# A fused complex-decay attention and feed-forward kernel: unit 0's attention reordered, stacking issued by two queues, one scale step moved

## The chip, the cores and the metric

The kernel runs on one core of one Trainium2 chip. The metric is device time of one execution in microseconds. A profiled execution adds a span, from its first to its last recorded instruction, and a trace of every engine: PE (matrix products), DVE and ACT (element-wise work), POOL, and SP, whose queue here only issues DMAs. ACT has a DMA queue of its own too.

## What is computed

```python
def _attn_ref(q, k, v, a_re, a_im):                  # [4, 8, 768, 48] each
    mag = np.sqrt(a_re * a_re + a_im * a_im)
    scale = np.minimum(mag, 0.999) / (mag + 1e-06)
    a_re_n, a_im_n = (a_re * scale, a_im * scale)
    for t in range(S):
        ar, ai = (a_re_n[:, :, t, :, None], a_im_n[:, :, t, :, None])
        new_re = ar * S_re - ai * S_im
        new_im = ar * S_im + ai * S_re
        kv = np.einsum('bhd,bhe->bhde', k[:, :, t], v[:, :, t])
        S_re, S_im = (new_re + kv, new_im)
        y[:, :, t] = np.einsum('bhd,bhde->bhe', q[:, :, t], S_re)

def _moe_ref(x, w_a, w_b, w_out):                    # x: the attention's output, 3072 x 384
    return ((x @ w_a) * (x @ w_b) @ w_out)           # 384 -> 1536 -> 384
```

## The kernel before

The recurrence is computed in chunks of 128 tokens. A **unit** is one chunk of two batches (256 tokens, eight heads of 48): 12 units, six chunks for each of two pairs of batches. For every unit `u` the program does this:

- `load_a(u)` brings the decays (`a_t`, one of two buffers), `load_qk(u)` the queries and keys, `load_v(u)` the values; all on SP's queue.
- `scale(u, a_t, tmp)` computes the factor by which the decays are scaled. It is a chain between ACT and DVE: squares (L178), a sum (DVE, L179), four transcendental passes and a square (ACT, L180 to L184), then DVE's L186, ACT's L187, and DVE's L189, L191 and L193. `tmp` is a tile whose contents are no longer needed. Five DVE passes in all.
- `prep(u)` multiplies the decays by that factor (L211), forms cumulative products of them (L227 to L302), and turns queries and keys into decayed ones: L318 to L324 for the keys, and twice L309, which ends it. It is a generator: the main loop draws pieces of it between products.
- `stack(u)` copies the result from `qk` into `stk`, one DMA per head (two heads straddle a 128-partition border and take two), ten in all. Heads 0 to 7 are issued in order.
- `attn(u)` works from `stk`, for each batch `i` of the two and each half `hg` of the heads: `scores` (L379, four products into a `pm` bank, then DVE's mask into a tile `am`, L382), `transposes` of the keys (L390, copied to `kt` by ACT, L394), `outputs` (L422, values times masked scores plus the carried state, into `xp`; ACT casts it to `xh`, L424), `residual` (what the cast lost, to `xl`: for units 0 and 1 by a product L432 and ACT's L435, later by DVE's L430), and `state` (L445 and L452 to L456, the carried state `us`).
- The feed-forward of unit `w` runs over 12 blocks `f` of the hidden width: `gemm1` is 18 products (L489) into a bank `ab`; ACT and DVE turn that into `hh` and `hl` (L497 to L500); `gemm2`, two blocks later, is six products (L507).

Before the loop, unit 0 is prepared alone, and the weights are converted to a pair of tiles each (`split_weights`: DVE's L134 to L138, ACT's L142 and L149, PE's L147 and L148), 36 pieces; what is left of them is spread over w=0. In iteration `w` of the main loop the products of unit `w`, attention of unit `w+1` and `prep` of later units are written interleaved; a scheduler that knows priorities (`tc.high_priority`) then fixes one order for each engine, and each engine and each DMA queue works through its own in order, waiting where an operand isn't there.

In `prep`, the scale of the next unit is drawn along with the rounds of the cumulative product: `prep(1)` runs scale(1) ahead of itself and scale(2) within its last rounds, `prep(2)` runs scale(3), and so on. The attention of unit 0 has an order of its own, written at the end of `attn`. The pools give `am` two buffers, `xh` and `xl` two, `pm` two banks, `ab` three.

Of the kernel before, what the change touches and what calls it, by code (L numbers as in the profile page):

```python
# [8 lines left out]
F32 = mybir.dt.float32  # L9
# [13 lines left out]
NU = NBP * NCH  # L23
# [17 lines left out]
RUN = 2 * TOK + 2  # L41
NF = DF // 128
KS = 2 * D
LAG = 2
HB = 3
OWN_FROM = 2
# [21 lines left out]
def tile_kernel(ctx: ExitStack, tc: tile.TileContext, a_d, qk_d, v_d, w_d, qn_d, kn_d, vn_d, an_d, out_d):  # L68
    nc = tc.nc
    vec, act, pe, sync = nc.vector, nc.scalar, nc.tensor, nc.sync  # L70
# [8 lines left out]
    kvp = fast.enter_context(tc.tile_pool(name="kvp", bufs=2))  # L79
# [26 lines left out]
    stk = const.tile([128, H, RUN], F32, name="stk")  # L106
    nc.gpsimd.memset(stk[KS:128], 0.0)
    qk = const.tile([128, NJ, 2, RUN], F32, name="qk")
# [46 lines left out]
    def load_a(u):  # L155
        t = apool.tile([128, 2, W], F32, name="a_t")
        for hs in halves if u == 0 else (slice(0, W),):
            sync.dma_start(out=t[:, :, hs], in_=a_d[u, :, :, hs])
        return t

    a_tiles = {}

    sc_tiles = {}
    halves = (slice(0, W // 2), slice(W // 2, W))
# [2 lines left out]
    def scale(u, a_t, tmp):  # L167

        sc = zpool.tile([128, W], F32, name="sc")
        for n, hs in enumerate(halves if u == 0 else (slice(0, W),)):
            n = n and NU
            t = tmp[:, 0:2, hs]
            m, x, s0 = t[:, 0], t[:, 1], sc[:, hs]
            act.activation(out=t, in_=a_t[:, :, hs], func=AF.Square, accum_out=sums[:, u + n:u + n + 1])  # L178
            vec.scalar_tensor_tensor(out=m, in0=m, scalar=-EPS * EPS, in1=x, op0=ALU.add, op1=ALU.add)  # L179
            act.activation(out=s0, in_=m, func=AF.Ln, bias=b_sq)  # L180
            act.activation(out=s0, in_=s0, func=AF.Exp, scale=0.5)
            act.activation(out=s0, in_=s0, func=AF.Ln, bias=b_eps)
            act.activation(out=s0, in_=s0, func=AF.Exp, scale=-1.0)
            act.activation(out=x, in_=s0, func=AF.Square)  # L184
            yield 900
            vec.tensor_tensor(out=m, in0=m, in1=x, op=ALU.mult)  # L186
            act.activation(out=x, in_=s0, func=AF.Identity, scale=-EPS, bias=b_one)  # L187
            yield 900
            vec.scalar_tensor_tensor(out=m, in0=m, scalar=-0.5, in1=x, op0=ALU.mult, op1=ALU.add)  # L189
            yield 900  # L190
            vec.scalar_tensor_tensor(out=s0, in0=m, scalar=0.5, in1=s0, op0=ALU.add, op1=ALU.mult)  # L191
            yield 900
            vec.scalar_tensor_tensor(out=s0, in0=s0, scalar=0.999, in1=x, op0=ALU.mult, op1=ALU.min)  # L193
            yield 900
        sc_tiles[u] = sc
# [4 lines left out]
    def prep(u):  # L200
        c = u % NCH
        a_t = a_tiles.pop(u)
        if u == 1:
            yield from scale(u, a_t, a_first)
            a_tiles[u + 1] = load_a(u + 1)
        sc = sc_tiles.pop(u)
        z = zpool.tile([128, 3, W], F32, name="z") if u else z_first
# [4 lines left out]
                              in1=sc.rearrange("p (b i e) -> p b i e", e=2, i=SUB // 2), op=ALU.mult)  # L212
        act.activation(out=z[:, 0], in_=z[:, 2], func=AF.Copy, scale=-1.0)
        yield 1700
        sg = scale(u + 1, a_tiles[u + 1], a_t) if 0 < u < NU - 1 else iter(())


        zb = z.rearrange("p s (j b e) -> p s j b e", j=SUB // 2, e=2)
# [5 lines left out]
        for i in range(1, SUB):  # L224
            pr = small.tile([128, 2, 2, NB], F32, name="pr", bufs=1)
            for o, n in parts:
                vec.tensor_tensor(  # L227
                    out=pr[:, :, :, o:o + n],
# [7 lines left out]
        for _ in sg:  # L236
# [9 lines left out]
            out=pt, in0=last2[1],  # L246
# [13 lines left out]
        for sb in range(0, NSB, 2):  # L260
            pb = small.tile([128, 2, 2, G], F32, name="pb")
            vec.tensor_tensor(  # L262
                out=pb,
# [9 lines left out]
            out=pt, in0=last2[0], in1=bv[:, 1:3, 0:NB:2].unsqueeze(1).broadcast_to([128, 2, 2, NB // 2]), op=ALU.mult)  # L273
# [12 lines left out]
        for k in range(2):  # L286
            pz = a_t
            for s in range(2):
                vec.tensor_tensor(  # L289
                    out=pz[:, s].rearrange("p (j b e) -> p j b e", j=SUB // 2, e=2), in0=zb[:, 1 + s],  # L290
# [38 lines left out]
        for k in range(2):  # L329
            times_p(k, 0 if u else 1, 2)  # L330
            yield 1670
        if 0 < u < NU - 2:
            a_tiles[u + 2] = load_a(u + 2)

    def load_qk(u):
        sync.dma_start(out=qk[:, :, 1, 0:2 * TOK], in_=qk_d[u])

    def stack(u):
        n = RUN if rescaled(u % NCH) else 2 * TOK
        for h in range(H):  # L340
            r0 = h * D
            while r0 < (h + 1) * D:
                j, p = divmod(r0, 128)
                m = min((h + 1) * D - r0, 128 - p)
                d0 = 2 * (r0 - h * D)
                sync.dma_start(out=stk[d0:d0 + 2 * m, h, 0:n], in_=qk[p:p + m, j, :, 0:n])
                r0 += m


# [12 lines left out]
                          (3 * g + 2, [(2 * g, 32), (2 * g + 1, 64)])):  # L362
            quads[q % 4].append((q // 4, [(h, g * 128 + off) for h, off in pieces]))

    def attn(u, xh, xl):

        c = u % NCH
        last = c + 1 == NCH
# [5 lines left out]
        def scores(i, hg):  # L374
            qs, ks = cols(i)
            sp = ps_m.tile([128, 4, 128], F32, name="pm")
            for h4 in range(4):
                h = hg * 4 + h4
                pe.matmul(out=sp[:, h4], lhsT=stk[:, h, ks], rhs=stk[:, h, qs], start=True, stop=True)  # L379
            am = kvp.tile([128, 512], F32, name="am", bufs=2).rearrange("p (h t) -> p h t", h=4)  # L380
            with tc.high_priority(offset=ATTN_FIRST):
                vec.tensor_tensor(out=am, in0=sp, in1=mask[:].unsqueeze(1).broadcast_to([128, 4, 128]),  # L382
                                  op=ALU.mult)
            ams[i, hg] = am

        def transposes(i, hg):
            qs, ks = cols(i)
            tp = ps_m.tile([128, 512], F32, name="pm")
            for h4 in range(4):
                pe.transpose(out=tp[:, h4 * KS:(h4 + 1) * KS], in_=stk[0:KS, hg * 4 + h4, ks],  # L390
                             identity=ident[0:KS, 0:KS])
            kt = kvp.tile([128, 4, KS], F32, name="kt", bufs=2)
            with tc.high_priority(offset=ATTN_FIRST):
                act.copy(out=kt.rearrange("p h k -> p (h k)"), in_=tp[:, 0:4 * KS])  # L394
            kts[i, hg] = kt
# [41 lines left out]
        def state(i, hg):  # L437
# [4 lines left out]
            for h4 in range(4):  # L442
                h = hg * 4 + h4
                o = (h // 2) * 128 + (h % 2) * (80 if own else 32)
                pe.matmul(out=kp[0:KS, h4 * n:(h4 + 1) * n], lhsT=kts[i, hg][:, h4, :],  # L445
                          rhs=v_t[:, o:o + n], start=True, stop=True)
# [3 lines left out]
            with tc.high_priority(offset=ATTN_FIRST):  # L450
# [4 lines left out]
                if rescaled(c):  # L455
                    vec.tensor_tensor(out=uv, in0=uv, in1=sv, op=ALU.mult)  # L456

        order = [(scores, 0, 0), (scores, 0, 1), (transposes, 0, 0), (transposes, 0, 1),
                 (outputs, 0, 0), (scores, 1, 0), (residual, 0, 0), (state, 0, 0), (scores, 1, 1),
                 (state, 0, 1), (transposes, 1, 0), (transposes, 1, 1), (outputs, 1, 0),  # L460
                 (state, 1, 0), (residual, 1, 0), (state, 1, 1)]
        if u == 0:
            order = [(scores, 0, 0), (scores, 0, 1), (outputs, 0, 0), (scores, 1, 0), (scores, 1, 1),
                     (residual, 0, 0), (outputs, 1, 0), (transposes, 0, 0), (transposes, 0, 1),
                     (residual, 1, 0), (state, 0, 0), (state, 0, 1), (transposes, 1, 0), (transposes, 1, 1),
                     (state, 1, 0), (state, 1, 1)]
        for fn, i, g in order:
            if not (last and fn in (transposes, state)):
                fn(i, g)
# [5 lines left out]
    def new_x():  # L475
        return (moe.tile([128, NJ, TOK], F32, name="xh"), moe.tile([128, NJ, TOK], F32, name="xl"))
# [126 lines left out]
                    sync.dma_start(out=out_v[bass.ds(c, 1), bp, tt].rearrange("o p m -> p (o m)"), in_=o_sb)  # L603


    a_first = a_tiles[0] = load_a(0)
    load_weights(0)
    load_qk(0)
    load_weights(1)
# [21 lines left out]
    p1 = prep(1)  # L631
    for _ in range(CONV_FIRST):
        next(ws)
    x_cur = new_x()
    for _ in attn(0, *x_cur):
        drain(p1, P1_A)
    pend = []

# [11 lines left out]
    for w in range(NU):  # L650
# [18 lines left out]
        for f in range(NF):  # L669
# [9 lines left out]
            slot()  # L679
            if len(pend) > LAG:  # L680
                second()
# [11 lines left out]
        x_cur = x_nxt  # L693
# [74 lines left out]
```

## Time and profile before

| | |
|---|---|
| median of 3 runs | 691.08 us (691.05 to 691.49) |
| the profiled execution | 690.18 us |
| its span | 688.5 us |
| PE busy | 644.5 us, 94% of the span |
| DVE busy | 550.1 us, 80% |
| ACT busy | 310.1 us, 45% |
| stack(0), stack(1), stack(2) start | 57.63, 121.20, 167.64 us |

Busy shares are averages over the span. Rows of the timeline give start, duration, engine, line, operation, output and inputs, and in brackets the idle time of the engine ahead of it with what ended it. An engine's next instruction can start a little before the one ahead of it ends. A product of 32-bit operands outside the feed-forward shows as two records.

### The profile page before, as it was taken

To read this page: it belongs to the slowest core of one execution; us is meant where nothing else is said; L and a number is where in the kernel's file an instruction comes from. 1 tells how busy PE (TensorE), PEld (TensorE's weight loads), DVE (VectorE), ACT (ScalarE), POOL (GpSimd) and SP (SyncE) were. 2 spreads that over 40 slices of the span, in tenths; PEclk is the share of its full clock that TensorE was granted. 3 is DMA by queue.
4 is the path that set the end of the run, shared out by engine and by line. 5 is a ranking of instruction groups with operands and counts; after the bars stand their busy time and mean duration, and the time that the engine had idled before them with its cause. 6 is when DMAs were issued, how large, how long until landed. Compare 5 with 4: busy or idle time off the path is not lost.

```text
span 688.5 us, 14290 instructions
## 1 busy us (share of the span) xinstructions
PE 644.5 (94%) x5842; PEld 608.3 (88%) x5842; DVE 550.1 (80%) x1259; ACT 310.1 (45%) x622; POOL 5.6 (1%) x11
## 2 busy tenths in 40 slices
PE   3547999999999999999999999999999999999996
PEld 1214889899999999999999999999999999999996
DVE  6999899998989989999898898999989963233221
ACT  7357664735445346354363553635542332221221
POOL 3000000000000000000000000000000000000000
PEclk9676999999999999999999999999999999999999
DMA  8963301513314225043160440611500500400000
GB/s 321 402 268 95 121 1 44 143 54 87 115 39 139 63 78 145 16 136 104 29 194 2 122 117 3 178 60 62 155 24 18 153 24 18 108 24 2 24 1 28
DMA packets 30232, 63.94 MB, mean 93 GB/s; under 512 B 3664, under 2 KB 7248, under 8 KB 30160
## 3 DMA queue, kind: packets, MB, share of 16 engines
q1 hardware_dynamic: 26704, 58.23, 27.3%
q10 hardware_dynamic: 3456, 4.72, 1.9%
q8 instruction: 48, 0.79, 0.5%
q14 instruction: 24, 0.20, 0.1%
HBM read 39.32 MB, written 4.72 MB: 64 GB/s over the span
## 4 chain that ended last, share of the span: by engine, by line
PE 66%; DVE 25%; ACT 4%; DMA 2%; issue 2%; SPq 0%; DVEq 0%; ACTq 0%
PE ab L489 33%; PE o L507 16%; PE xp L422 5%; PE pm L379 4%; PE pm L445 3%; DVE a_t L289 3%; DVE qk L309 2%; PE pm L390 2%; DVE h_t L498 2%; DVE hl L500 2%; PE pm L147 1%; DVE z L294 1%; DVE pr L227 1%; DVE am L382 1%; DVE pb L262 1%
## 5 line engine op out<-in xcount | busy, mean ns | idle before, releaser
L489 PE MATMUL ab<-xh,w 128*128 128x256 f32 x1728 | 341.6, 286 | 0.0
L489 PEld LDWEIGHTS ab<-xh,w 128*128 128x128 f32 x1728 | 277.2, 189 | 1.7 <-issue 0.8
L489 PE MATMUL ab<-xl,w 128*128 128x256 f32 x864 | 245.5, 284 | 0.0
L489 PEld LDWEIGHTS ab<-xl,w 128*128 128x128 f32 x864 | 163.0, 189 | 0.6 <-issue 0.2
L507 PE MATMUL o<-w,hh 128*128 128x384 f32 x576 | 152.7, 343 | 0.0
L497 ACT COPY h_t<-ab 128x256 f32<-128x256 f32 x144 | 53.4, 371 | 163.4 <-PE ab L489 163.4
L498 DVE TENSOR_TENSOR h_t<-ab,h_t 128x256 f32<-128x256 f32 x144 | 60.4, 420 | 64.6 <-ACT h_t L497 64.3
L507 PEld LDWEIGHTS o<-w,hh 128*128 128x128 f32 x576 | 96.6, 188 | 1.1 <-issue 1.0
L507 PE MATMUL o<-w,hl 128*128 128x384 f32 x288 | 97.2, 338 | 0.0
L499 ACT CAST hh<-h_t 128x256 fp32r<-128x256 f32 x144 | 58.0, 403 | 78.0 <-DVE h_t L498 76.9
L500 DVE TENSOR_TENSOR hl<-h_t,hh 128x256 fp32r<-128x256 f32 x144 | 60.4, 419 | 16.6 <-ACT hh L499 16.4
L379 PE MATMUL pm<-stk 128*128 128x128 f32 x384 | 54.8, 280 | 2.1 <-DMA stk<-qk 2.0
L147 PE MATMUL ab<-o_sb,ident 128*128 128x384 f32 x42 | 28.1, 764 | 29.7 <-DVE o_sb L138 29.7
L379 PEld LDWEIGHTS pm<-stk 128*128 128x128 f32 x384 | 50.2, 194 | 5.7 <-issue 3.6
L507 PEld LDWEIGHTS o<-w,hl 128*128 128x128 f32 x288 | 54.1, 188 | 0.0
L227 DVE TENSOR_TENSOR pr<-z 128x384 f32<-128x384 f32 (+1 forms) x91 | 47.2, 525 | 1.8
L289 DVE TENSOR_TENSOR a_t<-z,b_t 128x768 f32<-128x768 f32 x48 | 44.7, 947 | 0.1
L147 PEld LDWEIGHTS ab<-o_sb,ident 128*128 128x128 f32 x42 | 9.5, 268 | 39.3 <-DVE o_sb L138 30.3
L309 DVE TENSOR_TENSOR qk<-qk,z 128x1536 f32<-128x1536 f32 (+1 forms) x26 | 42.3, 1626 | 0.2
L422 PE MATMUL xp<-am,v_t 128*32 128x128 f32 x768 | 37.7, 281 | 4.3 <-DVE am L382 4.1
L382 DVE TENSOR_TENSOR am<-pm,mask 128x512 f32<-128x512 f32 x48 | 32.7, 685 | 5.2 <-PE pm L379 4.4
L424 ACT CAST xh<-xp 128x384 fp32r<-128x384 f32 x24 | 11.4, 475 | 49.3 <-PE xp L422 49.1
(107 smaller groups left out, 768.7 us busy)
## 6 DMA issues: line engine op xcount, KB each, us to landing
w<-in_dram SPq DMA_DIRECT2D x36, 384.0 KB, 8.0
qk<-in_dram SPq DMA_DIRECT2D x12, 768.0 KB, 4.9
stk<-qk SPq DMA_DIRECT2D x48, 192.0 KB, 3.3
a_t<-in_dram SPq DMA_DIRECT2D x11, 768.0 KB, 4.3
v_t<-in_dram SPq DMA_DIRECT2D x24, 256.0 KB, 2.7
stk<-qk SPq DMA_DIRECT2D x24, 192.8 KB, 3.3
out_dram<-o_sb ACTq DMA_DIRECT2D x24, 192.0 KB, 1.9
stk<-qk SPq DMA_DIRECT2D x16, 128.0 KB, 3.1
```

The source lines that it names most:

```text
L147: pe.matmul(out=lp[:, 0:n], lhsT=ident, rhs=t, start=True, stop=False)
L227: vec.tensor_tensor(out=pr[:, :, :, o:o + n], in0=view(zz, W + at_(i) + 2 * o, [[W, 2], [-W, 2], [2, n]]), in1=tok(slice(1, 3), i - 1, o, ...
L289: vec.tensor_tensor(out=pz[:, s].rearrange("p (j b e) -> p j b e", j=SUB // 2, e=2), in0=zb[:, 1 + s], in1=view(bb, (1 + k - s) * NB, [[0, ...
L309: vec.tensor_tensor(out=qk4[:, :, k, x0:x1], in0=qk4[:, :, 1, x0:x1], in1=z[:, k].rearrange("p (j t) -> p j t", j=NJ).unsqueeze(2).broadca ...
L379: pe.matmul(out=sp[:, h4], lhsT=stk[:, h, ks], rhs=stk[:, h, qs], start=True, stop=True)
L422: run = pe.matmul(out=xp[qd * 32:(qd + 1) * 32, ti], lhsT=l, rhs=rr, start=st, stop=sp_, tile_position=(0, qd * 32), skip_group_check=True ...
L489: pe.matmul(out=ab[:, m * TOK:(m + 1) * TOK], lhsT=r(w_ab(f, part, m * NJ + i)), rhs=r(xt[:, i, :]), start=n == 0, stop=n == 8)
L497: act.copy(out=h_t, in_=ab[:, 0:TOK])
L498: vec.tensor_tensor(out=h_t, in0=ab[:, TOK:2 * TOK], in1=h_t, op=ALU.mult)
L499: act.copy(out=r(hh), in_=h_t)
L500: vec.tensor_tensor(out=r(hl), in0=h_t, in1=hh, op=ALU.subtract)
L507: pe.matmul(out=os_[tt][:, 0:DM], lhsT=r(ht[:, ts]), rhs=r(w_t[f, 2][:, part, :]), start=(f == 0 and n == 0), stop=(f == NF - 1 and n == 2))
```

## The change

1. `stack(u)` for units 0 and 1 issues the DMAs of the odd heads on ACT's queue, and those of the even heads on SP's.
2. In unit 0's attention all four `scores` come first. Two more `am` tiles are needed for that; they are a pair of `xh` and `xl` tiles that nothing uses yet.
3. scale(2) moves from within prep(1) to the front of prep(2), behind unit 1's keys and queries. With it, `load_a(3)` moves from the end of prep(1) to a place behind scale(2), since scale(2) uses unit 1's decay tile as `tmp`. From scale(3) on nothing is changed.

```diff
+SCALE_LATE = 2
...
     def prep(u):
         c = u % NCH
         a_t = a_tiles.pop(u)
-        if u == 1:
-            yield from scale(u, a_t, a_first)
+        if 0 < u <= SCALE_LATE:
+            yield from scale(u, a_t, a_old.pop())
             a_tiles[u + 1] = load_a(u + 1)
...
-        sg = scale(u + 1, a_tiles[u + 1], a_t) if 0 < u < NU - 1 else iter(())
+        sg = scale(u + 1, a_tiles[u + 1], a_t) if SCALE_LATE <= u < NU - 1 else iter(())
...
-        if 0 < u < NU - 2:
+        if SCALE_LATE <= u < NU - 2:
             a_tiles[u + 2] = load_a(u + 2)
+        else:
+            a_old.append(a_t)
...
-                sync.dma_start(out=stk[d0:d0 + 2 * m, h, 0:n], in_=qk[p:p + m, j, :, 0:n])
+                eng = act if u < 2 and h % 2 else sync
+                eng.dma_start(out=stk[d0:d0 + 2 * m, h, 0:n], in_=qk[p:p + m, j, :, 0:n])
...
-            am = kvp.tile([128, 512], F32, name="am", bufs=2).rearrange("p (h t) -> p h t", h=4)
+            if (i, hg) in spare:
+                am = spare[i, hg].rearrange("p j t -> p (j t)")[:, 0:512].rearrange("p (h t) -> p h t", h=4)
+            else:
+                am = kvp.tile([128, 512], F32, name="am", bufs=2).rearrange("p (h t) -> p h t", h=4)
...
         if u == 0:
-            order = [(scores, 0, 0), (scores, 0, 1), (outputs, 0, 0), (scores, 1, 0), (scores, 1, 1),
-                     (residual, 0, 0), (outputs, 1, 0), (transposes, 0, 0), (transposes, 0, 1),
-                     (residual, 1, 0), (state, 0, 0), (state, 0, 1), (transposes, 1, 0), (transposes, 1, 1),
-                     (state, 1, 0), (state, 1, 1)]
+            order = [(scores, 0, 0), (scores, 0, 1), (scores, 1, 0), (scores, 1, 1),
+                     (outputs, 0, 0), (residual, 0, 0), (outputs, 1, 0), (residual, 1, 0),
+                     (transposes, 0, 0), (transposes, 0, 1), (state, 0, 0), (state, 0, 1),
+                     (transposes, 1, 0), (transposes, 1, 1), (state, 1, 0), (state, 1, 1)]
...
-    for _ in attn(0, *x_cur):
+    for _ in attn(0, *x_cur, {(1, 0): am_first[0], (1, 1): am_first[1]}):
```

The scheduler's order changes with it. Lines of the changed kernel stand 2 to 8 lower, so its L182 is L180 of before, its L390 is L382, and its L384 is L379. First ACT's order before, from the end of prep(1) on (L213 is the copy behind prep(2)'s first multiplications, L178 and L180 are scale(3)'s first passes):

```order
L497 COPY h_t<-ab 128x256
L213 ACTIVATE z<-z 128x768
L499 CAST hh<-h_t 128x256
L142 CAST w_1092<-o_sb 128x384
L178 ACTIVATE a_t,chk<-a_t 128x1536
L149 CAST w_1092<-pm 128x384
L394 COPY kt<-pm 128x384
L180 ACTIVATE sc<-a_t,biases 128x768
```

And the changed kernel's ACT order at the same place (L180, two rows ahead of these, and L182 are scale(2)'s first passes, L351 is the stacking of unit 1):

```order
L505 COPY h_t<-ab 128x256
L351 DMA stk<-qk 96x1x514
L507 CAST hh<-h_t 128x256
L351 DMA stk<-qk 96x1x514
L351 DMA stk<-qk 32x1x514
L505 COPY h_t<-ab 128x256
L351 DMA stk<-qk 64x1x514
L507 CAST hh<-h_t 128x256
L351 DMA stk<-qk 96x1x514
L182 ACTIVATE sc<-a_t,biases 128x768
L183 ACTIVATE sc<-sc 128x768
L402 COPY kt<-pm 128x384
```

Five issues now stand between scale(2)'s square and its second ACT pass, and the copies of `kt`, which belong to attn(1), between its further passes. Next DVE before, from the last L309 of prep(1):

```order
L309 TENSOR_TENSOR qk<-qk,z 128x3x512
L500 TENSOR_TENSOR hl<-h_t,hh 128x256
L498 TENSOR_TENSOR h_t<-ab,h_t 128x256
L138 SCALAR_TENSOR_TENSOR o_sb<-w_196,o_sb 128x384
L134 TENSOR_SCALAR o_sb<-w_198 128x384
L500 TENSOR_TENSOR hl<-h_t,hh 128x256
L136 SCALAR_TENSOR_TENSOR o_sb<-w_198,o_sb 128x384
L211 TENSOR_TENSOR z<-a_t,sc 128x96x4x2
```

And the changed kernel's DVE, eight rows behind the same L309 (L188 to L195 are scale(2)'s passes, L390 the masks of attn(1), L213 the first multiplication of prep(2)):

```order
L188 TENSOR_TENSOR a_t<-a_t 128x768
L390 TENSOR_TENSOR am<-pm,mask 128x512
L191 SCALAR_TENSOR_TENSOR a_t<-a_t 128x768
L460 TENSOR_TENSOR u_111<-pm,u_111 96x2x2x48
L390 TENSOR_TENSOR am<-pm,mask 128x512
L506 TENSOR_TENSOR h_t<-ab,h_t 128x256
L464 TENSOR_TENSOR u_111<-u_111,stk 96x2x2x48
L460 TENSOR_TENSOR u_111<-pm,u_111 96x2x2x48
L508 TENSOR_TENSOR hl<-h_t,hh 128x256
L464 TENSOR_TENSOR u_111<-u_111,stk 96x2x2x48
L193 SCALAR_TENSOR_TENSOR sc<-a_t,sc 128x768
L195 SCALAR_TENSOR_TENSOR sc<-sc,a_t 128x768
```

The multiplication that followed the end of prep(1) by seven rows now follows it by twenty, behind scale(2) and most of attn(1)'s share of DVE; it is the row after these. The last pieces of the weight conversion (L134 to L138 before) now stand ahead of that L309. Last PE before, at the first scores of unit 2 (L379; `w_873` and `w_883` are the weights of block f=8):

```order
L489 MATMUL ab<-xh,w_873 128x256
L379 MATMUL pm<-stk 128x128
L489 MATMUL ab<-xh,w_883 128x256
L489 MATMUL ab<-xl,w_883 128x256
L489 MATMUL ab<-xh,w_883 128x256 x2
L489 MATMUL ab<-xl,w_883 128x256
L379 MATMUL pm<-stk 128x128
```

And the changed kernel's PE at its first scores of unit 2 (L515 is `gemm2`, `w_1077` the last weight block of w=1, L398 the transposes):

```order
L515 MATMUL o_1588<-w_1077,hh 128x384 x2
L384 MATMUL pm<-stk 128x128
L515 MATMUL o_1588<-w_1077,hl 128x384
L515 MATMUL o_1589<-w_1077,hh 128x384 x2
L384 MATMUL pm<-stk 128x128
L515 MATMUL o_1589<-w_1077,hl 128x384
L384 MATMUL pm<-stk 128x128 x3
L398 MATMUL pm<-ident,stk 128x96 x5
L384 MATMUL pm<-stk 128x128
L398 MATMUL pm<-ident,stk 128x96
```

The scores of unit 2 stood among the blocks f=8 to f=10 of w=1 and now come behind f=11; behind them stand only the rest of attn(2) and then w=2, which needs its result. From unit 3 on the orders are nearly alike.

More of the change, by code (lines that the diff above doesn't have):

```diff
@@ L161, in tile_kernel @@
     a_tiles = {}
+    a_old = []
     sc_tiles = {}
@@ L363, in tile_kernel, with attn @@
             quads[q % 4].append((q // 4, [(h, g * 128 + off) for h, off in pieces]))
-    def attn(u, xh, xl):
+    def attn(u, xh, xl, spare={}):
         c = u % NCH
@@ L603, in feed_forward @@
                     sync.dma_start(out=out_v[bass.ds(c, 1), bp, tt].rearrange("o p m -> p (o m)"), in_=o_sb)
-    a_first = a_tiles[0] = load_a(0)
+    a_tiles[0] = load_a(0)
     load_weights(0)
@@ L633, in tile_kernel @@
         next(ws)
+    am_first = new_x()
     x_cur = new_x()
-    for _ in attn(0, *x_cur):
+    for _ in attn(0, *x_cur, {(1, 0): am_first[0], (1, 1): am_first[1]}):
         drain(p1, P1_A)
```

## The prediction

> **What bounds the kernel now.** I read the busy tenths of the page first, then busy time by stretch, then the timelines around the stretches where PE isn't full.
>
> ```profile
> PE   3547999999999999999999999999999999999996
> DVE  6999899998989989999898898999989963233221
> PEclk9676999999999999999999999999999999999999
> ```
>
> ```profile
> 40.00:60.00 20.00, 9.88 (x17) 4.32 (x17) 20.00 (x33) 11.23 (x18) 0.00 (x0) 0.56 0.35 128
> 60.00:80.00 20.00, 16.88 (x154) 13.78 (x154) 17.41 (x33) 13.33 (x27) 0.00 (x0) 0.84 0.54 162
> 80.00:120.00 40.00, 39.98 (x262) 35.34 (x261) 39.88 (x102) 25.08 (x55) 0.00 (x0) 1.00 0.07 22
> 120.00:167.60 47.60, 47.46 (x462) 45.21 (x461) 43.25 (x96) 23.60 (x46) 0.00 (x0) 1.00 0.31 92
> 167.60:200.00 32.40, 31.03 (x351) 30.14 (x350) 30.53 (x78) 14.87 (x29) 0.00 (x0) 1.00 0.32 91
> ```
>
> The columns are the stretch, its length, then busy time of PE, weight loads, DVE, ACT and POOL, the granted clock, DMA share and GB/s. From 80 us PE is full, so the time is the moment at which PE starts in earnest, plus its work, plus any later hole. Up to 120 us DVE is full as well (20.00 of 20, 39.88 of 40), and later it has under 10% to spare: whatever is late on DVE there stays late. That decides this case, because stack(2), which ends DVE's work for unit 2, is only just in time:
>
> ```profile
> 167.64 6.72 SPq L346 DMA_DIRECT2D stk<-qk  x10
> 177.20 0.60 SPq L336 DMA_DIRECT2D qk<-in_dram  x1
> 171.12 0.46 PE L379 MATMUL pm<-stk 128*128 128x128 f32 x2 [1.37 <-DMA stk<-qk]
> ```
>
> PE's first score of unit 2 waits 1.37 us for the first head; the load at 177.20 waits for the last one, 9.6 us after stack(2) begins.
>
> **Part 1, start of unit 0 (two queues, reordered attention).**
>
> ```profile
> 57.63 6.81 SPq L346 DMA_DIRECT2D stk<-qk  x10
> 67.23 0.60 SPq L336 DMA_DIRECT2D qk<-in_dram  x1
> L346 SPq DMA_DIRECT2D stk<-qk x10: 589/610/758, 57.6 to 63.8; - x10
> DMA to landing us min/median/max: 2.5/3.0/3.4
> L647 ACTq DMA_DIRECT2D out_dram<-o_sb x22: 338/338/417, 149.6 to 649.0; - x22
> 58.10 0.48 ACT L149 CAST w<-ab 128x384 fp32r<-128x384 f32 x1 [0.78 <-PE ab L148]
> 69.06 0.68 DVE L382 TENSOR_TENSOR am<-pm,mask 128x512 f32<-128x512 f32 x1
> 69.79 1.93 PE L422 MATMUL xp<-am,v_t 128*32 128x128 f32 x32 [2.22 <-DVE am L382]
> 71.79 0.48 ACT L424 CAST xh<-xp 128x384 fp32r<-128x384 f32 x1 [2.11 <-PE xp L422]
> 73.56 0.69 DVE L382 TENSOR_TENSOR am<-pm,mask 128x512 f32<-128x512 f32 x1 [0.69 <-PE pm L379]
> 74.40 1.08 PE L422 MATMUL xp<-am,v_t 128*32 128x128 f32 x32 [0.36 <-DVE am L382]
> 81.78 0.28 PE L489 MATMUL ab<-xh,w 128*128 128x256 f32 x1
> ```
>
> Ten issues take 6.81 us and the last lands at 67.2. Split, SP's five end near 61; ACT's five start behind the cast at 58.10, at 58.6. No row has a stacking issue on ACT: between 0.34 (its stores) and 0.76 (SP's slowest) I take SP's median 0.61, nearest in kind, so the last issues end at 61.6 and land at 64.5, 2.7 us sooner. The Trainium skill ("DMA: Bandwidth & Descriptors", section "Issuing engines are not separate DMA queues") says that two issuers share the same 16 DMA engines and save only issue time, usually small beside the transfer. Here the rows put 6.81 us of issue against 3.0 to landing; if the rule's "small" held, part 1 would lose its 2.7 us.
>
> ACT pays: scale(1)'s L180 starts at 61.6 instead of 58.5. From there I follow the queues: the second mask is done at 65.4 (was 69.74), the first L422 group ends at 67.0, ACT reaches xh at 68.2 (was 71.79), the fourth mask ends at 69.9 (was 74.25), the second L422 group at 71.0. The 18th L489, with all of attn(0) behind it, ends at 77.4 instead of 82.06: **-4.7 us for PE**, between -6 and -2. DVE gains only 0.15 us: its first L211 of unit 1 still waits for scale(1) through ACT.
>
> **Part 2, scale(2) behind unit 1's keys.** It takes five DVE passes out of prep(1) and puts them, with seven ACT passes, ahead of prep(2)'s first multiplication.
>
> ```profile
> 119.43 1.75 DVE L309 TENSOR_TENSOR qk<-qk,z 128x1536 f32<-128x1536 f32 x1
> 121.77 0.55 DVE L138 SCALAR_TENSOR_TENSOR o_sb<-w,o_sb 128x384 uint32<-128x384 uint32 x1
> 122.23 0.35 DVE L134 TENSOR_SCALAR o_sb<-w 128x384 uint32<-128x384 uint32 x1
> 125.41 0.95 DVE L211 TENSOR_TENSOR z<-a_t,sc 128x768 f32<-128x768 f32 x1
> 128.93 0.95 DVE L179 SCALAR_TENSOR_TENSOR a_t<-a_t 128x768 f32<-128x768 f32 x1
> 140.97 0.95 DVE L193 SCALAR_TENSOR_TENSOR sc<-sc,a_t 128x768 f32<-128x768 f32 x1
> 130.35 0.94 ACT L180 ACTIVATE sc<-a_t,biases 128x768 f32<-128x768 f32 x1
> 134.85 0.85 ACT L184 ACTIVATE a_t<-sc 128x768 f32<-128x768 f32 x1
> 137.57 0.35 DVE L452 TENSOR_TENSOR u<-pm,u 96x192 f32<-96x192 f32 x1
> 147.74 0.42 DVE L498 TENSOR_TENSOR h_t<-ab,h_t 128x256 f32<-128x256 f32 x1
> 165.87 1.75 DVE L309 TENSOR_TENSOR qk<-qk,z 128x1536 f32<-128x1536 f32 x1
> ```
>
> (a) prep(1) ends at 121.18. After: minus 0.15, minus five passes of 0.95 (4.7), plus what is pulled ahead of its end, the last four passes of the weight conversion (L138 twice, L134, L136; 0.55+0.35+0.55+0.55 = 2.0): **118.3**.
>
> (b) In the row order of before, scale(3) takes 13.0 us from L179 at 128.93 to the end of L193 at 141.92, hidden under prep(2). Scale(2) now runs with nothing of prep(2) beside it. Its L179 starts at 118.7, but on ACT the five stacking issues of unit 1 stand between the square and L180, and they wait for 118.3 themselves: with two evacuation pairs among them L180 starts at 122.4. L180 to the end of L184 takes 5.35 us in the rows; two copies of kt now sit in it and wait for transposes of the last head (landing near 125.5), +1.3. L186 to L193 takes 6.2; two masks in it wait for scores, +0.8. So scale(2) ends at 136.0 and the second L211 at 137.8, where before it ended at 126.36.
>
> (c) From there to the end of L309 before: 167.62 - 126.36 = 41.3. After: four masks (0.68) and four state updates (0.35) fewer, three and a half h_t and hl pairs (0.84) more, 40.1; passes start some 0.08 closer than they last, so 39.5. **Stack(2) starts at 177.3** instead of 167.6. Ends: 172.6 if the chain takes its old 13.0 us, 179.5 if nothing of the 41.3 is saved.
>
> (d) What stands behind it. The order moves unit 2's scores on PE behind all of w=1's products: 3.5 more blocks of L489 and 5.3 more of L507.
>
> ```profile
> 186.62 1.89 PE xp L422 x64
> 188.51 0.81 PE pm L390 x8
> 195.05 2.20 PE ab L489 x18
> 197.25 1.05 PE o L507 x6
> ```
>
> PE arrives there at 171.12 - 1.37 + 3.5 x 2.2 + 5.3 x 1.05 - 4.7 = 178.3. The first head lands at 177.3 + 3.0, the last at 177.3 + 9.6; no product is left to fill that. Before, the second L422 group ended 20.9 us after stack(2) started, and after that L424 (0.48), DVE's residual and the semaphores cost 2.1 more, so w=2's first full block starts at 177.3 + 23.0 = 200.3. Before, the same state was reached at 195.05 + 2 x 1.05 (two L507 blocks of w=1 still to come) + 0.25 for two odd L489 = 197.4: **+2.9 us**. The 4.7 us won at the start are inside this: PE spends them waiting.
>
> (e) The clock. Attn(2) alone leaves PE about half idle for 20 us, as it was in 40 to 60 (9.88 of 20, granted 0.56). The first L422 group took 1.93 us there-abouts against 1.08 for the second, the same 32 passes. I take +0.6, from nothing to +5 (the two L422 groups and two score groups at half speed). The Trainium skill ("TensorE: Matmul & The Clock Gate", "Part 1: The HAM clock gate") says the clock halves after an idle window of some 3.4 us. The 0.56 agrees; by that rule a hole of that length ahead of the last head would bring the upper price.
>
> The spare masks in new_x's tiles, load_a(3) behind scale(2) (needed only in the last rounds of prep(2), some 4 us later) and later units, whose order is nearly the old one, I cost at nothing; if stack(3) inherits the delay, 1 to 2 us more.
>
> **Sum:** +2.9 + 0.6 = +3.5 on the profiled execution's 690.18 (span 688.5), 693.7. The median shown is 691.08, 0.9 above it: **694.5**. Against 691.08, 0.2% (1.4 us) is about what a measurement can tell from no change.
>
> **Rivals.** (1) *Stack(2) is in time, faster.* With a start below about 170 PE finds all heads, and attn(2) costs only its own waits: a mask (0.68) ahead of the first transposes and of each L422 group and a copy or cast (0.48) at three places, some 3.3 us with their semaphores, instead of the 1.37 of before: -4.7 + 1.9 = -2.8, **688.3**. For it: DVE has passes to give and the prologue gain is real work moved. Against: the chain in (b) would have to lose 7 us. Chance 0.2. (2) *A draw.* The change is T + 23.0 - 197.4 for a start T of stack(2), zero at 174.4, within the bounds of (c): **691**. Chance 0.2. (3) *The clock falls in attn(2).* For it: the 0.56. Against: scores come every 0.7 us, so no hole is very long. +8, **699**. Chance 0.12. (4) *Two queues don't do what they say*: stack(1)'s heads come no sooner, scale(2) waits for them too, T + 1 and **695.5**. Against: 6.81 us of issue. Chance 0.06. Forecast: 0.42.
>
> The range 687 to 698 leaves out the far half of (1) and most of (3); the forecast's own is 692.5 to 697. Faster by over 0.2%: 0.2. Within: 0.2. Slower: 0.6, from (3), (4) and the forecast.
>
> **What would show it.** Right: the 18th L489 near 77.4; prep(1)'s last L309 ending near 118; L180 of scale(2) four microseconds after its L179; stack(2) starting at 175 to 179; an idle PE between 178 and 200 put down to the stacking DMAs and to the masks; PE full again after. Wrong: stack(2) before 172, or PE full from 178 to 190. The prologue step is wrong if attn(0) doesn't move by 2 to 6 us.

## The result and the profile after

The changed kernel takes **699.98 us** (median of 4, 697.51 to 701.26) where the kernel before takes 691.07 (median of 4): a ratio of 1.0124, 95% interval 1.0096 to 1.0152. It is slower, as forecast, but by 8.9 us and not by 3.5, above the range. The profiled execution took 701.26 us with a span of 699.5, 11.0 above the span of before; these two executions lie further apart than the medians.

The busy tenths on the page of the changed kernel, to be held against those of before:

```profile
PE   3547999899899999999999999999999999999996
DVE  6996999499998998989989899898999983233221
PEclk9666999999889999999999999999999999999999
```

Two dents in PE are new, the eighth slice (122 to 140 us) and the eleventh (175 to 192), and two in DVE, the fourth (52 to 70) and again the eighth. The same places by stretch (columns as in the prediction):

```profile
60.00:80.00 20.00, 18.68 (x163) 14.69 (x163) 13.90 (x23) 12.88 (x27) 0.00 (x0) 0.77 0.48 125
120.00:140.00 20.00, 17.59 (x190) 16.30 (x189) 10.39 (x18) 9.74 (x18) 0.00 (x0) 1.00 0.48 120
180.00:190.00 10.00, 7.81 (x47) 6.55 (x45) 9.89 (x15) 4.92 (x10) 0.00 (x0) 0.93 0.62 183
190.00:200.00 10.00, 8.65 (x89) 7.19 (x90) 8.94 (x18) 6.11 (x9) 0.00 (x0) 0.56 0.57 175
```

DVE, the engine that must not be late, loses 3.5 us of work between 60 and 80 (13.90 against 17.41 before). Between 120 and 140 it does 10.39 us of work; before it did 19.00 there:

```profile
120.00:140.00 20.00, 19.86 (x198) 17.96 (x200) 19.00 (x39) 12.80 (x23) 0.00 (x0) 1.00 0.46 132
```

The start first. From the timeline of the changed kernel, ACT and its queue, then DVE, then PE (L182 and L185 are passes of scale(1), L150 and L143 the weight conversion, L390 a mask, L213 prep(1)'s first multiplications):

```profile
57.73 5.82 ACTq L351 DMA_DIRECT2D stk<-qk  x5
63.60 0.93 ACT L182 ACTIVATE sc<-a_t,biases 128x768 f32<-128x768 f32 x1 [5.45 <-DMA stk<-qk]
70.17 0.48 ACT L150 CAST w<-ab 128x384 fp32r<-128x384 f32 x1 [3.25 <-PE ab L149]
70.55 0.85 ACT L185 ACTIVATE sc<-sc 128x768 f32<-128x768 f32 x1
...
66.03 0.69 DVE L390 TENSOR_TENSOR am<-pm,mask 128x512 f32<-128x512 f32 x1 [4.27 <-PE pm L384]
69.33 0.69 DVE L390 TENSOR_TENSOR am<-pm,mask 128x512 f32<-128x512 f32 x1 [1.16 <-PE pm L384]
78.25 1.83 DVE L213 TENSOR_TENSOR z<-a_t,sc 128x768 f32<-128x768 f32 x2
...
66.99 2.97 PE L384 MATMUL pm<-stk 128*128 128x128 f32 x16
69.72 0.59 PE L149 MATMUL ab<-w,nident 128*128 128x384 f32 x2
81.15 0.28 PE L497 MATMUL ab<-xh,w 128*128 128x256 f32 x1
```

ACT stands still for 5.82 us while it issues five DMAs. Then it meets the conversion's cast L150, which needs L149 on PE. That is queued behind eight scores (sixteen records), which stand behind late heads (PE waits 1.12 us for one) and run at a granted clock of 0.50 up to 69 us: 3.25 us more for ACT. DVE waits 4.27 us at the first mask. prep(1)'s multiplications begin at 78.25, where they began at 74.17, and the 18th product ends at 81.43, hardly sooner than the 82.06 of before.

The second stacking and what follows (L181 to L195 are scale(2), the last row nine of the ten issues of SP's stack(2)):

```profile
120.67 1.75 DVE L311 TENSOR_TENSOR qk<-qk,z 128x1536 f32<-128x1536 f32 x1
123.00 0.95 DVE L181 SCALAR_TENSOR_TENSOR a_t<-a_t 128x768 f32<-128x768 f32 x1
127.29 0.94 ACT L182 ACTIVATE sc<-a_t,biases 128x768 f32<-128x768 f32 x1 [0.27 <-issue]
132.46 0.48 ACT L402 COPY kt<-pm 128x384 f32<-128x384 f32 x1 [3.36 <-PE pm L398]
135.80 0.96 DVE L188 TENSOR_TENSOR a_t<-a_t 128x768 f32<-128x768 f32 x1 [2.03 <-ACT a_t L186]
142.13 0.96 DVE L195 SCALAR_TENSOR_TENSOR sc<-sc,a_t 128x768 f32<-128x768 f32 x1
143.13 1.83 DVE L213 TENSOR_TENSOR z<-a_t,sc 128x768 f32<-128x768 f32 x2
184.00 6.05 SPq L351 DMA_DIRECT2D stk<-qk  x9
```

Stack(2) begins at 184.00 instead of 167.64. PE has by then only the last of `gemm2` of w=1 left (to 189.1). Then it runs attention of unit 2 alone, and for a while at the lower clock (0.56 in 190 to 200):

```profile
187.51 0.46 PE L384 MATMUL pm<-stk 128*128 128x128 f32 x2 [0.48 <-DMA stk<-qk]
195.97 0.66 PE L430 MATMUL xp<-am,v_t 128*32 128x128 f32 x8 [0.62 <-DVE am L390]
203.36 0.43 PE L430 MATMUL xp<-am,v_t 128*32 128x128 f32 x8 [0.40 <-DVE am L390]
207.75 0.39 PE L497 MATMUL ab<-xl,w 128*128 128x256 f32 x1
```

At 207.75 the first full block of w=2 gets going; in the terms of the prediction the same state was reached at 197.4 before. These 10.4 us are nearly all of the 11.0 between the spans.

### The profile page after: what moved, and what is told of

The parts are those of the page before. It is cut to its first block, busy times and chain, and to the rows that moved or that the text cites. A ratio compares the mean times of both kernels' runs of the same rounds, so it can differ in the third digit from the quotient of the medians.

```text
span 699.5 us, 14279 instructions
## 1 busy us (share of the span) xinstructions
PE 650.8 (93%) x5842; PEld 612.4 (88%) x5842; DVE 551.4 (79%) x1259; ACT 311.5 (45%) x622; POOL 5.6 (1%) x11
## 4 chain that ended last, share of the span: by engine, by line
PE 58%; DVE 26%; DMA 9%; ACT 4%; issue 2%; SPq 1%; DVEq 0%; ACTq 0%
PE ab L497 28%; PE o L515 12%; PE xp L430 6%; DMA w<-in_dram 5%; PE pm L384 5%; DMA stk<-qk 3%; PE pm L453 3%; DVE qk L311 3%; DVE h_t L506 2%; PE pm L398 2%; DVE hl L508 2%; DVE pr L229 2%; DVE a_t L291 1%; DVE z L235 1%; PE pm L148 1%
## 5 line engine op out<-in xcount | busy, mean ns | idle before, releaser
L515 PE MATMUL o<-w,hh 128*128 128x384 f32 x576 | 151.0, 342 | 1.1 <-ACT hh L507 1.1
L506 DVE TENSOR_TENSOR h_t<-ab,h_t 128x256 f32<-128x256 f32 x144 | 60.5, 420 | 60.9 <-ACT h_t L505 60.4
L515 PE MATMUL o<-w,hl 128*128 128x384 f32 x288 | 98.6, 343 | 0.2 <-DVE hl L508 0.2
L515 PEld LDWEIGHTS o<-w,hh 128*128 128x128 f32 x576 | 96.7, 188 | 2.1 <-ACT hh L507 1.4
L508 DVE TENSOR_TENSOR hl<-h_t,hh 128x256 fp32r<-128x256 f32 x144 | 60.5, 420 | 18.6 <-ACT hh L507 18.5
L384 PE MATMUL pm<-stk 128*128 128x128 f32 x384 | 59.5, 292 | 5.9 <-DMA stk<-qk 5.8
L384 PEld LDWEIGHTS pm<-stk 128*128 128x128 f32 x384 | 52.6, 202 | 11.8 <-DMA stk<-qk 5.2
L515 PEld LDWEIGHTS o<-w,hl 128*128 128x128 f32 x288 | 54.1, 188 | 1.2 <-DVE hl L508 0.5
L390 DVE TENSOR_TENSOR am<-pm,mask 128x512 f32<-128x512 f32 x46 | 31.5, 686 | 14.5 <-PE pm L384 14.4
```

The costliest lines, as they stand in the source:

```text
L506: vec.tensor_tensor(out=h_t, in0=ab[:, TOK:2 * TOK], in1=h_t, op=ALU.mult)
L508: vec.tensor_tensor(out=r(hl), in0=h_t, in1=hh, op=ALU.subtract)
L515: pe.matmul(out=os_[tt][:, 0:DM], lhsT=r(ht[:, ts]), rhs=r(w_t[f, 2][:, part, :]), start=(f == 0 and n == 0), stop=(f == NF - 1 and n == 2))
```

## The experiments

In the diffs, + and - stand against the changed kernel or, where it says so, the kernel before. Where a time is said to be so much after stack(0) begins, it is because that moment itself lies up to 2 us apart in the profiles (57.44 to 59.40). Ratios are to executions of the kernel before that ran beside it, with their 95% intervals.

**The three edits taken apart.** One queue, the rest as changed:

```diff
-                eng = act if u < 2 and h % 2 else sync
+                eng = sync
```

> The changed kernel with all stacking issues back on SP's queue (reordered attention of unit 0 and late scale(2) kept). Theory A (ACT stands behind its own five issues for some 5 us, twice, and DVE inherits it through the scale chains): L182 of scale(1) starts near 58.5 instead of 63.60, the first L213 of unit 1 near 75.5 instead of 78.25, L182 of scale(2) under 2 us behind its L181 instead of 4.3, stack(2) at 175 to 179 instead of 184.0, median 691 to 695. Rival B (the late scale(2) alone makes stack(2) late, the queues are beside the point): stack(2) at 182 to 185, median 698 to 700.

The time is 692.49 us, ratio 1.0027 (1.0016 to 1.0039): three quarters of the loss go with the second queue. Theory A holds, B falls; stack(2), at 173.4, comes even sooner than A's 175 to 179. The timeline of this kernel:

```profile
58.98 6.74 SPq L351 DMA_DIRECT2D stk<-qk  x10
59.85 0.94 ACT L182 ACTIVATE sc<-a_t,biases 128x768 f32<-128x768 f32 x1
66.22 0.69 DVE L390 TENSOR_TENSOR am<-pm,mask 128x512 f32<-128x512 f32 x1
73.39 1.82 DVE L213 TENSOR_TENSOR z<-a_t,sc 128x768 f32<-128x768 f32 x2
117.61 0.94 DVE L181 SCALAR_TENSOR_TENSOR a_t<-a_t 128x768 f32<-128x768 f32 x1
118.67 0.94 ACT L182 ACTIVATE sc<-a_t,biases 128x768 f32<-128x768 f32 x1
```

L182 follows stack(0)'s begin by 0.9 us and not by 6.2, the mask has no wait ahead of it, and scale(2)'s L182 follows L181 by 1.06 us and not by 4.29.

Scale(2) back in prep(1), two queues and the new order kept:

```diff
-SCALE_LATE = 2
+SCALE_LATE = 1
```

> The changed kernel with scale(2) back inside prep(1) (two queues and reordered attention kept). Theory A: the start still costs DVE about 3 to 4 us, so stack(1) starts near 124 to 125 (121.20 before), stack(2) near 171 (167.64), and the median is 692 to 695. Rival B: with scale(2) in its old place the time is that of before less the gain on PE, 689 to 691.

696.81 us, ratio 1.0096 (1.0072 to 1.0121). Theory A's direction is right and its size too small: stack(1) begins at 126.58, stack(2) at 176.53. The late scale is not the main loss.

The kernel before with one edit each. First the late scale alone (against the changed kernel the old order of unit 0 and one queue):

```diff
-            order = [(scores, 0, 0), (scores, 0, 1), (scores, 1, 0), (scores, 1, 1),
+            order = [(scores, 0, 0), (scores, 0, 1), (outputs, 0, 0), (scores, 1, 0), (scores, 1, 1),
...
-                eng = act if u < 2 and h % 2 else sync
+                eng = sync
```

> The kernel before with only scale(2) moved (one queue, old order of unit 0). Theory A: start as before (first L211 of unit 1 near 74.2), stack(1) near 118, stack(2) at 173 to 176, median 691 to 695. Rival B: the move alone gives nearly the whole loss, median 697 to 700.

695.68 us, ratio 1.0067 (1.0050 to 1.0084), a little above theory A's band: stack(1) begins at 117.70 and stack(2) at 176.79.

The reordered attention alone:

```diff
-SCALE_LATE = 2
+SCALE_LATE = 1
...
-                eng = act if u < 2 and h % 2 else sync
+                eng = sync
```

> The kernel before with only unit 0's attention reordered. Theory A: the heads land as before (last near 67.2), the 18th product of the first block ends between 79 and 81.5 (82.06 before), and the median is 689.5 to 691.5. Rival C (all four scores ahead of the weight conversion's L149 on PE stop ACT, which waits there for 3.25 us in the changed kernel, and scale(1) with it): the first L213 of unit 1 starts 1 to 3 us later than 74.17, and the median is 691.5 to 694.

688.93 us, ratio **0.9976 (0.9966 to 0.9986)**, faster than both kernels and than either theory. Its first L213 comes 15.3 us after stack(0) begins (16.5 before), so rival C falls: without the second queue the scores ahead of L149 stop nobody. The 18th product ends 23.1 us after stack(0) begins, where it was 24.4 before.

The second queue alone:

```diff
-SCALE_LATE = 2
+SCALE_LATE = 1
...
-            order = [(scores, 0, 0), (scores, 0, 1), (scores, 1, 0), (scores, 1, 1),
+            order = [(scores, 0, 0), (scores, 0, 1), (outputs, 0, 0), (scores, 1, 0), (scores, 1, 1),
```

> The kernel before with only the second queue for stack(0) and stack(1). Theory A (ACT stands still for its own five issues, scale(1) with it): scale(1)'s L182 starts 5 to 6 us behind its L181 instead of 1, the first L213 of unit 1 18.5 to 21 us after stack(0) begins (16.5 before), stack(2) 117 to 120 us after it (110.0 before), median 695 to 699. Rival E (the queues hurt only together with the reordered attention, whose scores stand ahead of the weight conversion on PE): first L213 within 1 us of before, median 690.5 to 692.5.

695.95 us, ratio 1.0066 (1.0049 to 1.0082). All of theory A's numbers are met (L182 6.0 us behind L181, L213 at 20.3, stack(2) at 118.8); rival E falls. The queue, with the order that the scheduler makes for it, hurts by itself.

Put on one after another, the order stands at -0.24%, with the late scale at +0.27%, with the second queue at +1.24%. In microseconds of 691 these are steps of -1.7, +3.5 and +6.7. Alone, the three are worth -0.24%, +0.67% and +0.66%, in sum +1.09%, so they come near to adding up.

**Where the second queue hurts.** For stack(0) alone, and in the next kernel for stack(1) alone:

```diff
-                eng = act if u < 2 and h % 2 else sync
+                eng = act if u < 1 and h % 2 else sync      # stack(1) alone: u == 1
```

> The changed kernel with the second queue for stack(0) alone. Theory A: the first L213 of unit 1 stays near 20 us after stack(0) begins, stack(1) near 65, and stack(2) follows stack(1) by about 57 us as with one queue (61.6 in the changed kernel): near 122 after stack(0) (126.6 changed, 114.4 with one queue); median 695 to 698. If unit 0 carries nothing of the loss, 692 to 693.

> The changed kernel with the second queue for stack(1) alone. Theory A: the start as with one queue (first L213 14 to 15 us after stack(0) begins, stack(1) near 57 to 58), then stack(2) 59 to 62 us behind stack(1), since scale(2)'s L182 waits 4 us behind ACT's issues; median 693.5 to 697. If unit 1 carries nothing of the loss, 692 to 693.

For stack(0) alone: 694.53 us, ratio 1.0068 (1.0044 to 1.0093), L213 at 18.1 and stack(2) 56.2 us behind stack(1), as with one queue; the start is delayed, by 2 us less than theory A said, and the time is just below its band and above the 692 to 693 of no loss. One of its seven executions took 699.96 us, the others 694.24 to 695.75; the medians alone give a ratio of 1.0050. For stack(1) alone: 696.58 us, ratio 1.0065 (1.0040 to 1.0090), a start like that with one queue (L213 at 14.5), and stack(2) 61.5 us behind stack(1) instead of 57.1. Its rows show the reason, L182 6.88 us behind the L181 that feeds it:

```profile
116.53 2.08 ACTq L351 DMA_DIRECT2D stk<-qk  x2
116.61 0.95 DVE L181 SCALAR_TENSOR_TENSOR a_t<-a_t 128x768 f32<-128x768 f32 x1
118.74 2.20 ACTq L351 DMA_DIRECT2D stk<-qk  x2
123.49 0.95 ACT L182 ACTIVATE sc<-a_t,biases 128x768 f32<-128x768 f32 x1
```

Each place costs stack(2) a delay of 4.1 or 4.5 us against one queue (118.5 and 118.9 against 114.4 after stack(0) begins), both together 12.2. Why both together cost 3.6 us more than their sum was not tried.

**ACT standing still, or the transfers?** The odd heads on POOL's queue in place of ACT's, for both units:

```diff
-                eng = act if u < 2 and h % 2 else sync
+                eng = nc.gpsimd if u < 2 and h % 2 else sync
```

> The changed kernel with the odd heads issued by POOL's queue in place of ACT's: two queues still, but ACT issues nothing. Theory A (what costs is that ACT stands still): L182 of scale(1) 1 us behind L181, first L213 14 to 16 us after stack(0) begins (20.8 in the changed kernel, 14.4 with one queue), median 691.5 to 695. Rival D (two queues interleave the transfers and bring every head later, and that is what costs): first mask 8 us or more after stack(0) begins, first L213 18 us or more, median 697 to 700.

697.49 us, ratio 1.0084 (1.0061 to 1.0107): rival D's numbers, not A's.

```profile
58.62 6.26 SPq L351 DMA_DIRECT2D stk<-qk  x5
58.90 2.80 POOL L351 DMA_DIRECT2D stk<-qk  x5 [52.55 <-DVE qk L311]
59.49 0.94 ACT L182 ACTIVATE sc<-a_t,biases 128x768 f32<-128x768 f32 x1 [0.29 <-DVE a_t L181]
67.13 1.20 PE L384 MATMUL pm<-stk 128*128 128x128 f32 x4 [2.12 <-DMA stk<-qk]
68.43 0.69 DVE L390 TENSOR_TENSOR am<-pm,mask 128x512 f32<-128x512 f32 x1 [4.58 <-PE pm L384]
```

ACT is free at once, and still DVE waits 4.58 us for the first mask, which comes 9.8 us after stack(0) begins and not 7.2. Ahead of it PE waits 2.12 us for a head. The DMAs of SP's own queue land late too: 6.7 us after their issue (median), where it was 3.0 before. And the opposite, all ten issues of stack(0) on ACT, so that there is one queue and nothing is interleaved:

```diff
-                eng = act if u < 2 and h % 2 else sync
+                eng = act if u < 1 else sync
```

> The changed kernel with all ten issues of stack(0) on ACT's queue and stack(1) on SP's alone: one queue for the transfers, so nothing is interleaved, but ACT issues ten. Theory A (ACT's standing still is a cost of its own): L182 of scale(1) 7 us or more behind L181, first L213 of unit 1 20 to 23 us after stack(0) begins (18.1 with five on ACT, 14.4 with none), median 695 to 698. Rival D (only the interleaving costs): first L213 at 14 to 16 us, median 692 to 693.5.

702.17 us, ratio 1.0158 (1.0141 to 1.0175), the slowest of all. Theory A's moments are met, and the time lies 4 us above its band:

```profile
58.38 6.93 ACTq L351 DMA_DIRECT2D stk<-qk  x10
65.35 0.94 ACT L182 ACTIVATE sc<-a_t,biases 128x768 f32<-128x768 f32 x1 [6.56 <-DMA stk<-qk]
80.97 1.83 DVE L213 TENSOR_TENSOR z<-a_t,sc 128x768 f32<-128x768 f32 x2
```

So both are costs of their own: an ACT that issues is an ACT that does not compute (L213 at 22.6), and two queues bring the heads no sooner (L213 at 19.0, with ACT free).

**Why the heads come no sooner.** Two kernels made from the one before, each executed once, for the trace alone. In one, the DMAs of stack(0) and stack(1) are cut in two; in the other stack(1) copies half the columns.

```diff
+                m = min(m, D // 2) if u < 2 else m
```

> The kernel before with the DMAs of stack(0) and stack(1) cut in two, 18 issues for the same bytes on SP's one queue. If issuing sets the pace (what the prediction took: 0.61 us an issue): about 11 us of issues, the last transfer landing near 13.5 us after stack(0) begins, the DMA share in between about 0.5. If the transfer itself sets it: the share stays at 0.8 or more, and the last bytes are moved within 9.5 us as before (8.6).

```diff
-        stk[d0:d0 + 2 * m, h, 0:n], in_=qk[p:p + m, j, :, 0:n]
+        stk[d0:d0 + 2 * m, h, n0:n], in_=qk[p:p + m, j, :, n0:n]     # n0 = TOK for u == 1
```

> The kernel before where stack(1) copies only the columns of the keys, ten issues for half the bytes; unit 1's queries are left out, so its result is that of other queries. If issuing sets the pace: ten issues still take 6.5 to 7.1 us (7.11 before), landing 2.3 us or more later each. If the transfer sets it: each lands 1 us or more sooner than the 3.0 us of before, and the share of the DMA engines stays near 0.8 for about half as long.

The issues of stack(0) in the first, on SP's queue, and the stretch in which they run:

```profile
57.99 14.59 SPq L352 DMA_DIRECT2D stk<-qk  x18
```

```profile
58.00:72.00 14.00, 7.94 (x30) 5.08 (x30) 13.67 (x25) 9.40 (x17) 0.00 (x0) 0.81 0.46 97
```

And the issues of stack(1) in the second (ns, min/median/max) with their time to landing, and the stretch:

```profile
L352 SPq DMA_DIRECT2D stk<-qk x10: 576/592/832, 122.6 to 129.0; - x10
DMA to landing us min/median/max: 2.0/2.2/2.4
```

```profile
123.00:131.00 8.00, 7.56 (x49) 6.45 (x48) 7.50 (x15) 5.60 (x11) 0.00 (x0) 1.00 0.39 101
```

With more issues the share falls to 0.46 and the time doubles; at 0.81 us an issue it is longer than the 11 us expected from 0.61. With half the bytes the ten issues take as long as before (0.592 us each, median) at a share of 0.39. On one queue it is the issue that sets the pace, as I had taken it. Only the landing is 1 us shorter with half the bytes (2.2 against 3.2). But that pace is near the other limit already. Two slices of a microsecond of the kernel before, the same two of the changed one, and its time to landing:

```profile
63.00:64.00 1.00, 1.00 (x5) 0.62 (x5) 0.39 (x2) 1.00 (x3) 0.00 (x0) 1.00 0.75 232
64.00:65.00 1.00, 1.00 (x8) 0.82 (x6) 0.96 (x3) 1.00 (x3) 0.00 (x0) 1.00 0.83 223
```

```profile
63.00:64.00 1.00, 1.00 (x3) 0.92 (x4) 0.00 (x0) 0.40 (x1) 0.00 (x0) 0.50 1.06 199
64.00:65.00 1.00, 1.00 (x3) 0.48 (x2) 0.00 (x0) 1.00 (x3) 0.00 (x0) 0.50 1.02 262
```

```profile
DMA to landing us min/median/max: 3.5/5.0/5.5
```

In these slices one queue keeps the DMA engines at 0.75 to 0.83 of their time, two at 1.0. Over the whole transfer it is 0.82 at 217 GB/s with one queue (59 to 66 us) and 1.02 at 241 GB/s with two (60 to 65): a ninth more. The ten issues end 6.1 us after the first begins instead of 6.8, and the load that waits for the last head starts 9.25 us after stack(0) begins instead of 9.60. For this 0.35 us the median DMA takes 5.0 us to land instead of 3.0.

**Does the order on DVE matter?** In the changed kernel the first mask stands ahead of five passes of the weight conversion that stand ahead of it with one queue: the fixed order puts it where heads from two queues were due. Here one queue, and the conversion's passes from the 22nd piece on held behind the mask:

```diff
+                with ExitStack() as behind:
+                    if 3 * f + m >= 21:
+                        behind.enter_context(tc.issue_after(mask0[0]))
```

> The changed kernel with one queue, as in the first experiment, but the weight conversion's passes from its 22nd piece on held behind unit 0's first mask on DVE, which is where the scheduler puts them when it counts on two queues. Theory F (part of the loss with two queues is this order: the mask stands ahead of five conversion passes and DVE waits there for the heads): DVE idle 2 to 3 us ahead of the first mask (none with one queue), first L213 of unit 1 at 15.5 to 17 us after stack(0) begins (14.4), median 693.5 to 695.5. If the order is harmless: first L213 within 0.5 us of 14.4, median 692 to 693.

```profile
67.21 0.69 DVE L395 TENSOR_TENSOR am<-pm,mask 128x512 f32<-128x512 f32 x1 [4.47 <-PE pm L389]
```

DVE now waits 4.47 us ahead of this mask with one queue too, L213 comes at 16.8 instead of 14.4, and stack(2) 3.4 us later. So the order alone explains a part of what DVE loses. No head holds PE up here: from 60.5 us to this mask it never waits for one. What differs is its granted clock:

```profile
64.00:67.00 3.00, 3.00 (x11) 2.21 (x10) 0.00 (x0) 1.63 (x4) 0.00 (x0) 0.53 0.78 209
```

With one queue and the usual order it is 1.00 from 65 us on. In the traces the clock reaches 1.00 5.3 us after stack(0) begins with one queue, 8.4 with this order, 11.7 in the changed kernel and 13.9 with POOL. Late heads, the order and the clock come together at the start, and no run here takes all three apart. Measured from the 16.8 of this kernel, L213 comes 2.2 us later with POOL and 5.8 with ten issues on ACT; as the rest of DVE's order is not the same in those kernels, these are no exact shares.

The time, 693.10 us, ratio 1.0020 (1.0008 to 1.0032), can't be told from the 1.0027 of the first experiment. In the two profiled executions, though, it is 2.3 us longer from stack(0) to the end. Theory F is right about DVE; whether its delay of stack(2) is paid stays open.

The start, the stacking and the end of all kernels, each from one profile, in microseconds after stack(0) begins; the ratio is that of all executions:

| kernel | first L213 (L211) of unit 1 | stack(1) | stack(2) | end of the span | ratio |
|---|---|---|---|---|---|
| before | 16.5 | 63.6 | 110.0 | 630.9 | 1 |
| order only | 15.3 | 62.4 | 109.4 | 630.1 | 0.9976 |
| one queue | 14.4 | 57.3 | 114.4 | 631.2 | 1.0027 |
| mask first | 16.8 | 61.5 | 117.8 | 633.5 | 1.0020 |
| scale only | 16.8 | 58.3 | 117.4 | 635.7 | 1.0067 |
| queue for stack(0) | 18.1 | 62.3 | 118.5 | 633.8 | 1.0068 |
| queue for stack(1) | 14.5 | 57.4 | 118.9 | 636.9 | 1.0065 |
| queues only | 20.3 | 69.9 | 118.8 | 636.9 | 1.0066 |
| scale early | 18.8 | 68.5 | 118.4 | 636.5 | 1.0096 |
| POOL | 19.0 | 63.1 | 122.9 | 638.3 | 1.0084 |
| changed | 20.8 | 65.0 | 126.6 | 642.1 | 1.0124 |
| all on ACT | 22.6 | 69.3 | 125.5 | 641.6 | 1.0158 |

Roughly, whoever has stack(2) late ends late, as the prediction argued. But with stack(2) at 117.4 to 118.9 the ends lie up to 3.4 us apart, so it is not the whole of it.

## Why the prediction was right in part

The sign was right and so was the path through stack(2). The size was not: the time lies 2 us above the range.

**What bounds the kernel: right.** What is late on DVE up to stack(2) is paid on PE: the dents at 122 and 175 us and the 10.4 us at w=2's first block.

**Part 1, the step that failed.** The prediction had "the last issues end at 61.6 and land at 64.5, 2.7 us sooner", and from it -4.7 us for PE and DVE "0.15 us" sooner. Measured: ACT's last issue ends at 63.55, the last head gains 0.35 us and not 2.7, the 18th product ends at 81.43 (gain 0.6, not 4.7), and prep(1)'s first multiplications end at 80.08, 4.1 us *later* than before. Three things were wrong in it.
- I saw that issuing sets the pace, which the kernels with more issues and with half the bytes confirm, and took it that the transfer has room beside it. I had a row for the rate over 20 us (162 GB/s, share 0.54) but did not look at the seven microseconds themselves, where the share was 0.8. Two queues could gain a fifth at most. They gained a ninth in rate, and gave it back in time to landing. The Trainium skill's "DMA: Bandwidth & Descriptors", section "Issuing engines are not separate DMA queues", which I set aside, says that DMAs of several issuers interleave on the same 16 engines; the share of 1.0 and the 5.0 us agree with it. The Trainium skill's "Perfetto Trace Analysis", section "DMA Optimizations", says that balancing over several issuing engines may help if descriptor generation is the bottleneck, the engine looking busy with it as opposed to actual DMA time. SP looked busy (6.81 us without a longer gap), but the DMA time was there too, at a share of 0.82, and the edit alone did not help (ratio 1.0066), nor did POOL's queue in place of ACT's (1.0084 against 1.0027 with one queue).
- I priced ACT's issues at 0.61 us and their delay as hidden. Five took 5.82 us: each lasted 0.58 to 1.05 us, and 1.7 us passed between the fourth and the fifth. That they wait for the engines that both queues fill would fit, but no run shows it. Behind them stood scale(1), on which DVE waits.
- The orders put the masks and scores where early heads were due. Where heads are late, DVE and PE wait in them, and PE's L149 and ACT's L150 behind. PE's clock, which I did not price at the start, stayed at 0.50 up to 69 us beside it; what part of the delay is the clock's stays open.

**Part 2 (a): the echo of it.** prep(1) ends at 122.42, not 118.3: the 4.1 us are those of part 1. With one queue the five passes' 4.7 us came roughly: stack(1) begins 57.3 us after stack(0), 62.4 with scale(2) inside, and 0.9 of these 5.1 us are the sooner first L213.

**(b): mis-sized by 3.0 us.** From prep(1)'s end to that of scale(2) I had 17.7 us; it took 20.67. L182 came 4.9 us behind prep(1)'s end (4.1 predicted); the rest is the copy of kt that waits 3.36 us for transposes of late heads, where I had allowed 1.3 for two.

**(c): right.** 39.0 us from the second L213's end to stack(2), 39.5 predicted. Stack(2) at 184.00 against 177.3 is thus 4.1 + 3.0 - 0.5, within rounding. (The upper end of (c), with nothing of the 41.3 saved, adds up to 179.1 and not to 179.5.)

**(d) and (e): right.** For a stack(2) at T, w=2's first full block was to start at T + 23.0 and 0.6 for the clock; it started at T + 23.75. The clock did fall to 0.56, at the low price: with one queue, where it stays at 1.00, the 18th product of w=2 comes 25.8 us after stack(2) begins, as in the changed kernel.

**The rivals.** In mechanism (4), "two queues don't do what they say", came true; I gave it 0.06 and priced it at T + 1, because I had looked only at stack(1) and not at what the same failure does to DVE at the start. (1) and (2) needed a stack(2) that DVE never got. (3) named the fall of the clock, but at a price that wasn't paid.

The late scale cost 3.5 us on top of the new order (0.51%) and 4.6 alone (0.67%). That the sum of (d) and (e) is also +3.5 is chance: it stands for all three edits and a stack(2) at 177.3, and with one queue stack(2) began at 173.4. The reordering alone was worth -1.7 us of the time and 1.3 us at the 18th product, not the 4.7 that I gave it there together with the queues.

## What to carry to other kernels

Before splitting issues over two queues, read the DMA share in the very microseconds of the transfer: at 0.8 there was little to win here (0.35 us for the last head), however solid the issuing queue looked. An engine that also computes pays for each issue with its own time, and in a fixed order everybody behind it pays too. Where three edits come together, measure each alone: here one of them was a gain of 0.24% that the other two hid.

## What was not expected of the hardware

- A smaller DMA was not cheaper to issue: 18 issues of half the rows took 14.59 us, 0.81 each, against 0.68 (6.81 for ten) of the full ones.
- With two queues an issue itself gets slower: on ACT 0.583 to 1.047 us, on SP up to 1.212, where SP alone needed 0.589 to 0.758. With POOL as the second queue POOL's own issues took 0.588 to 0.657, and SP's beside them up to 2.906.
- PE's granted clock in the first microseconds of attention depends on what stands around it: it was 0.50 in 63 to 65 us of the changed kernel and 1.00 in the same stretch before, and sixteen of PE's score records took 2.97 us, where fourteen took 1.72 before. What exactly raises it was not tried.
